# Chunk 2's first product by half products, a second order written out from slot 27 on, and stores on SyncE

## The chip, the cores and the metric

The kernel runs on one core of a Trainium2 chip. The metric is the device time of one execution in microseconds (us), the median of several runs. Below, PE is TensorE (matmuls), PEld its weight loads, DVE VectorE, ACT ScalarE, POOL GpSimd and SP SyncE; SP computes nothing and issues most of the DMAs.

## The reference

Two layers, one after the other. First a linear attention over q, k and v of shape (8 batches, 8 heads, 576 positions, 64):

```
r(x)   = max(x, 0)
phi(x) = [r(x) * cos(w_s), r(x) * sin(w_s)]        # w_s = pi/2 * s/576, 128 features
kv  = sum_s phi(k)^T v        z = sum_s phi(k)
x   = (phi(q) kv) / (phi(q) z + 1e-6)
```

Its result, with the heads side by side, is x of 4608 rows by 512. Then a gated layer with w_in (512 x 2048), beta (2048) and w_out (2048 x 512):

```
h   = x w_in
g   = h * sigmoid(beta * h)
out = g w_out
```

The output is 4608 x 512 in float32. Matmuls are in bf16 with float32 sums.

## The kernel before

**The stages.** The rows of x come in 9 chunks of 512 (number c). A batch of the attention has 576 rows, so nine blocks of 64; chunk c holds eight blocks and needs batches c and c - 1 or so. For a batch: `q_relu`, `k_relu` (L195, L199) take the ReLU of the loaded tiles, `v_scale` (L202) makes v times cos and v times sin, `kv_mm` (L270) multiplies K with V on TensorE and `kv_take` (L281) copies the result to SBUF. `q_turn_dma` (L258) transposes q by a DMA on SyncE; `q_tan` or `tan_mul` (L263, L222) multiply it by a tangent, on GpSimd or VectorE. `num_mm` (L290) makes numerators and denominators, `x_div` (L337) divides on VectorE (three short instructions, L308 to L319), and `x_turn_dma` (L365) transposes three blocks of x into the tile xt by DMAs on SyncE. For chunk 1, `x_turn_pe` (L351) transposes them on TensorE instead.

**h and out, in two ways.** Chunk c has 16 column tiles of h (jt 0 to 15). The plain way, `h_group` (L413), is four 512-column matmuls by tile (L386) and the activation by ScalarE (L394), in a bank of PSUM that holds all 512 columns. The argument `cols` of `h_mm` (L380) cuts the second to fourth of these four into narrower ones. The other way is a Strassen-like scheme with seven products where eight blocks would be multiplied (the Winograd form). `fast_ops` (L464) gives its pieces. In an order's text they are letters: 1, 5, 6, 2, 7, 3, 4 are products on TensorE; c is a copy of the first product by ScalarE to a second bank (the seed); d or D a copy to SBUF by ScalarE or VectorE; e and f are additions on VectorE; A, B, X, Y, P, Q, U, V take a finished bank. `h_pair` (L504) uses it for two column tiles of h, each product being two matmuls of 256 columns (L511); it needs four differences of xt (`x_sum`, L450) and four of w_in (`wh_sum`, L436), made by VectorE. `o_pair` (L612) uses it for half of a chunk's out, each product eight matmuls of 256 columns (L621); it needs sums of g (`g_sum`, L397, tiles S1 to S4) and differences of w_out (`w_sums`, L874). `o_fast` (L556) is an older form of the same for chunk 1 alone.

**Who uses which.** Chunk 0: h plain, out plain (`o_part`, L553). Chunk 1: h plain, out by `o_fast`. Chunk 2: h plain (`h_first`, L1037), out by `o_pair`. Chunks 3 to 8: h by `h_pair`, out by `o_pair`. The first 16 slots of the loop at L854 are chunk 0's h, slots 16 to 31 its out; `early` (L807) puts attention work at certain slots, `rest` (L763) among them at slot 4.

**What sets the order.** The kernel writes its order out by hand; every engine works through its own instructions in the order in which they are issued, and semaphores make it wait for data of another. Chunk 1 is written as Python (L882 to L936). From chunk 2's out on, a text for each chunk (`ORDERS`, L938) names one piece after another, and `chunk` (L993) issues them. In it, besides the products: s is a sum of g, t of x, W of w_in; K the K and V product, kt and kT its copy; N numerators, x the division and transpose; v, w, k, q the scaling and ReLUs of the batches ahead; g the tangent on GpSimd; TQ the transpose of q; L a load.

**SyncE's queue.** SyncE issues loads, transposes and some stores in program order; an issue that waits holds up all behind it. `store` (L532) sends 128 rows of out in two DMAs of 64 rows; for chunks 0 to 6 GpSimd issues them (L535).

The four stage tiles of 128 x 2048 floats hold w_in, then w_out as loaded; after that `wx_tiles` (L422) takes them for the differences of w_in (w and v), of xt (x) and for one tile of tangents (q).

## Time and profile before

| | |
|---|---|
| runs | 273.32, 273.35, 274.3 us; median 273.35 |
| span of the profiled execution | 272.7 us |
| of the runs' median outside that span | 0.7 us |
| TensorE clock granted | full, to three figures, in the stages from 20 to 242 us |
| DMA | 54.00 MB moved, 198 GB/s over the span |
| SyncE's queue and GpSimd's queue, share of 16 DMA engines | 59.1% and 9.6% |
| DMA issues of out by GpSimd | 58 of 128 KB, 4.5 us each to landing |
| DMA issues of out by SyncE | 10 of 128 KB, 2.4 us each to landing |

The profile is of one execution. A busy time is the union of an engine's instructions; matmuls overlap, so a TensorE that is busy all the time isn't one at its peak, and the price of a matmul is better taken from a run of many, its length divided by their number. VectorE's instructions overlap at their ends too: from one start to the next is less than the busy time of one. The chain that ended last is followed back from the end, at each step to what released the instruction. The list of waits names who waited for whom, with the sum, the count and the longest; a row of the table by stage has the length of the stage, then busy time (and instructions) of PE, PEld, DVE, ACT and POOL, the granted clock, the share of DMA engines and GB/s. A timeline row has start, length, engine, line, operation, tiles, shapes, count, and in brackets the idle time before it with who ended it.

### The profile page before, as it was taken

What the parts mean: (1) busy time and instruction counts of PE and PEld (TensorE: products, weight loads), DVE (VectorE), ACT (ScalarE), POOL (GpSimd) and SP (SyncE); (2) the same over time, 40 slices, a digit from 0 to 9 for tenths busy, and PEclk for the clock granted to TensorE, in tenths of its full rate; (3) what the DMA queues carried; (4) which work ended last, traced back from release to release, by engine and by line L of the source; (5) the groups of instructions that cost most, each with busy time, mean ns of one, the idle gap of its engine ahead of it and who ended that gap; (6) DMA issues with size and microseconds to landing.
All of it is one profiled execution on the core that took longest, in us unless ns stands there. A gap on an engine that the chain in (4) does not pass through costs nothing.

```text
span 272.7 us, 8970 instructions
## 1 busy us (share of the span) xinstructions
PE 265.3 (97%) x3712; PEld 206.8 (76%) x3712; DVE 224.0 (82%) x596; ACT 188.4 (69%) x384; POOL 68.3 (25%) x89
## 2 busy tenths in 40 slices
PE   8899999999899999999999999999999999999994
PEld 8554455455784588888888888888888888888883
DVE  5989969499989889789989997899589768757852
ACT  4778777796419656899489966996696179428920
POOL 1444000510078000660085009300840060000001
PEclk9999999999999999999999999999999999999999
DMA  6999999999969999994589439943600570015005
GB/s 237 374 395 383 392 390 319 379 201 336 284 130 311 240 348 226 240 313 103 147 216 370 92 58 223 332 71 62 181 2 2 61 185 1 2 27 130 0 2 155
DMA packets 50681, 54.00 MB, mean 198 GB/s; under 512 B 31232, under 2 KB 31760, under 8 KB 50640
## 3 DMA queue, kind: packets, MB, share of 16 engines
q1 hardware_dynamic: 47504, 45.55, 59.1%
q0 software_dynamic: 2784, 7.61, 9.6%
q8 instruction: 29, 0.48, 0.7%
q10 hardware_dynamic: 352, 0.27, 0.4%
q14 instruction: 12, 0.10, 0.1%
HBM read 36.71 MB, written 9.44 MB: 169 GB/s over the span
## 4 chain that ended last, share of the span: by engine, by line
PE 85%; DVE 9%; DMA 3%; SPq 1%; issue 1%; ACT 1%; DVEq 0%
PE ps L621 32%; PE ps L511 27%; PE ps L386 10%; PE ps L544 5%; PE ps L563 4%; PE ps L297 3%; DMA raw_v<-in_v_dram 3%; PE ps L276 3%; DVE vb L219 1%; DVE xs L319 1%; DVE qs L223 1%; SPq L79 1%; DVE S L406 1%; DVE rk L193 1%; DVE qb L193 0%
## 5 line engine op out<-in xcount | busy, mean ns | idle before, releaser
L537 POOL DMA_DIRECT2D out_dram<-o_sb x58 | 33.9, 591 | 147.3 <-ACT o_sb L658 86.3
L420 ACT ACTIVATE g_t<-ps,beta 128x512 bf16<-128x512 f32 x96 | 60.3, 702 | 1.4 <-PE ps L511 1.3
L621 PEld LDWEIGHTS <-S 128*128 128x128 bf16 x448 | 43.4, 98 | 5.2
L511 PE MATMUL ps<-w_stage 128*128 128x256 bf16 x288 | 46.6, 272 | 0.1
L386 PE MATMUL ps<-xt,win 128*128 128x512 bf16 (+1 forms) x196 | 42.8, 375 | 0.1
L511 PEld LDWEIGHTS <-w_stage 128*128 128x128 bf16 x384 | 37.3, 98 | 5.1 <-issue 0.2
L487 DVE TENSOR_TENSOR ps<-ps,p 128x256 f32<-128x256 f32 x74 | 30.5, 428 | 8.6 <-PE ps L511 3.0
L394 ACT ACTIVATE g_t<-ps,beta 128x512 bf16<-128x512 f32 x48 | 32.3, 688 | 7.2 <-PE ps L386 7.1
L621 PEld LDWEIGHTS <-g_t 128*128 128x128 bf16 x336 | 32.3, 98 | 4.5 <-ACT g_t L420 0.4
L386 PEld LDWEIGHTS <-win 128*128 128x128 bf16 x196 | 18.7, 98 | 21.1 <-issue 0.5
L511 PE MATMUL ps<-xt,win 128*128 128x256 bf16 x192 | 32.9, 273 | 0.0
L511 PEld LDWEIGHTS <-win 128*128 128x128 bf16 x288 | 28.0, 98 | 3.4
L621 PE MATMUL ps<-wout,g_t 128*128 128x256 bf16 x224 | 28.9, 273 | 0.0
L406 DVE TENSOR_TENSOR S<-g_t 128x512 bf16<-128x512 bf16 (+1 forms) x66 | 25.7, 418 | 3.3 <-ACT g_t L420 1.7
L480 ACT COPY ps<-ps 128x256 f32<-128x256 f32 x62 | 22.6, 383 | 7.5 <-PE ps L621 4.0
L217 ACT ACTIVATE vb<-raw_v,sin 128x256 bf16<-128x256 f32 (+1 forms) x58 | 26.0, 503 | 1.5 <-DMA raw_v<-in_v_dram 1.5
L621 PE MATMUL ps<-T,S 128*128 128x256 bf16 x224 | 26.6, 273 | 0.0
L621 PE MATMUL ps<-wout,S 128*128 128x256 bf16 x224 | 26.4, 273 | 0.0
L319 DVE TENSOR_TENSOR xs<-ps,rden 128x768 bf16<-128x768 f32 (+4 forms) x26 | 22.8, 884 | 0.9 <-DVE rden L312 0.2
L223 POOL TENSOR_TENSOR qs<-qt,tanr 128x1152 bf16<-128x1152 bf16 x6 | 14.3, 2387 | 27.4 <-PE ps L563 21.0
L658 ACT COPY o_sb<-ps 128x512 f32<-128x512 f32 x11 | 6.3, 587 | 20.1 <-PE ps L621 20.1
L487 DVE TENSOR_TENSOR ps<-ps,u 128x256 f32<-128x256 f32 x36 | 15.3, 427 | 5.3 <-PE ps L511 3.3
(112 smaller groups left out, 414.7 us busy)
## 6 DMA issues: line engine op xcount, KB each, us to landing
raw_v<-in_v_dram SPq DMA_DIRECT2D x7, 1152.0 KB, 9.7
raw_k<-in_k_dram SPq DMA_DIRECT2D x7, 1152.0 KB, 9.5
raw_q<-in_q_dram SPq DMA_DIRECT2D x7, 1152.0 KB, 7.4
out_dram<-o_sb POOLq DMA_DIRECT2D x58, 128.0 KB, 4.5
w_stage<-in_moe_w_in_dram SPq DMA_DIRECT2D x3, 1024.0 KB, 12.8
w_stage<-in_moe_w_out_dram SPq DMA_DIRECT2D x2, 1024.0 KB, 7.9
w_stage<-in_moe_w_out_dram SPq DMA_DIRECT2D x4, 512.0 KB, 11.9
out_dram<-o_sb SPq DMA_DIRECT2D x10, 128.0 KB, 2.4
```

The lines of the kernel that those rows point to most:

```text
L217: got = nc.scalar.activation(o, a, AF.Copy, scale=t[:, n : n + 1])
L223: return eng.tensor_tensor(dst.rearrange("q n (g p) -> q n g p", g=2), src.rearrange("q n (g p) -> q n g p", g=2), tanr[:, n0:n1].unsqueez ...
L319: nc.vector.tensor_tensor(o.rearrange("q j n s d -> q j (n s) d"), nv[:, :, a:z, :, 0:D].rearrange("q j n s d -> q j (n s) d"), rden[:, :, ...
L386: nc.tensor.matmul(ps[:, h_bank(c, jt), i * 64 : (i + w) * 64], lhsT=win[jt // 4][:, mi, (jt % 4) * P : (jt % 4 + 1) * P], rhs=xt[:, i : i ...
L394: return nc.scalar.activation(gs[c, jt // 4][:, jt % 4], ps[:, h_bank(c, jt)], AF.Silu, scale=beta[:, jt : jt + 1])
L406: return nc.vector.tensor_tensor(o, l, r, op=op)
L420: return nc.scalar.activation(gs[c, jt // 4][:, jt % 4], bank, AF.Silu, scale=beta[:, jt : jt + 1])
L480: return nc.scalar.copy(at("a", 0), at("b", 0))
L487: nc.vector.tensor_tensor(dst, at("b", 0), st["p5"], op=ALU.add)
L511: nc.tensor.matmul(dst, lhsT=l[:, g], rhs=r[:, :, g * HP : (g + 1) * HP], start=start and g == 0, stop=g == 1, skip_group_check=True)
L537: (eng or own).dma_start(out=out_v[bb, n][:, m0:m1], in_=o_sb[hf * HP : (hf + 1) * HP, m0:m1])
L621: nc.tensor.matmul(dst, lhsT=l(i), rhs=r[:, i], start=start and i == 0, stop=i == order[-1], skip_group_check=True)
```

## The change

- Chunk 2's h is made by `h_pair`, as in chunks 3 to 8. `wh_sum` now takes four column tiles at once (two pairs), so there are 16 instructions of 512 elements where there were 32 of 256. Six of them are issued in `rest`, ahead of batch 1's q ReLU; the tiles for them are taken there.
- Chunk 1's out is made by `o_pair` in place of `o_fast`.
- The loop of slots ends at 26. Slots 27 to 31 (in the text S with the tile's number; R is chunk 1's transpose on TensorE), the whole of chunk 1 (G is a plain group of h, M a difference of w_out, Z the last numerators of batch 1) and all chunks after it are texts in `ORDERS`. A number and a slash ahead of a piece mean that it belongs to another chunk, so that the end of one chunk's out stands among the beginning of the next one's h; @ names a batch. The text of every chunk is new.
- More of the ReLUs and scalings for batches ahead are single pieces that either ScalarE or VectorE takes (v, z, k, r on ScalarE; w, u, l, q on VectorE).
- Slots 5 to 11 of chunk 0's h pass `cols=2`: 21 matmuls of 512 columns become 42 of 256.
- Stores of chunks 0 to 6 are issued by SyncE in place of GpSimd.

By instructions: 512-column matmuls of h fall by 85 and 256-column ones rise by 154; GpSimd issues 2 stores in place of 58, SyncE 66 in place of 10 (besides the halves at the very end).

```diff
-            h_group(0, slot)
+            h_group(0, slot, 2 if 5 <= slot < 12 else 1)
...
-            own = (nc.gpsimd if c < 7 or (c == NTC - 1 and tt == 0) else
-                   (nc.sync, nc.scalar)[hf] if c == NTC - 1 and tt % 2 else nc.sync)
+            own = (nc.sync if c < NTC - 1 else nc.gpsimd if tt == 0 else (nc.sync, nc.scalar)[hf] if tt % 2 else nc.sync)
...
         v_scale(1, 1, n0=8)
         k_relu(1, 0, 2)
+        wx_tiles("wv")
+        for sl, kind in ((0, 1), (0, 3), (0, 2), (0, 4), (1, 1), (1, 3)):
+            wh_sum(sl, kind)
         q_relu(1, 0)
...
+    def wh_sum(sl, kind):
+        A11, A12, A21, A22 = (
+            win[sl][:, 2 * jp : 2 * jp + 2].rearrange("q g (u r f) -> q g u r f", u=2, r=2)[:, :, :, r]
+            for r in range(2) for jp in range(2))
+        s1, s2, s3, s4 = (w_sum(sl, i) for i in range(4))
...
-    for slot in range(32):
+    for slot in range(27):
...
+        0: (
+            "W23 W33 W12 Sb W21 R0 Sc Sd 1/q0@2 R1 1/M1 1/M2 1/r1@2 Se Sf 1/u5@2 1/TQ@2"),
+        1: (
+            "G0 w6@2 z7@2 M4 w1@2 G1 M3 G3 0/W31 z8@2 w3@2 G4 G2 w2@2 w0@2 u3@2 w5@2 G9 u8@2 u0@2 Gb v2@2 Ge u6@2 s10 "
+            "G8 z4@2 Lq@3 u4@2 s20 kk@2 v1@2 Gf 0/W32 u7@2 G5 Ga Z6 K02 K1 Lv@3 Gc s12 kT G7 G6 y1 y0 s40 Gd s11 N05 "
+            "N13 ox17 oy12 oxc0 r1@3 x0 oyc1 x1 ox2 s13 s22 r0@3 ox5 oy5 Lk@3 TQ oyd v7 oxd s31 z7 N23 s32 v0 s21 s42 "
+            "z4 s23 s41 oy2 w1 oy6 x2 oye ox6"),
         2: (
+            "h215 1/v6 1/s43 1/v3 1/t1 h014 1/z5 1/Lq@4 1/v8 1/t2 1/s30 1/s33 1/z6 1/oxe 0/W14 1/w2 0/W22 h113 1/oy3 "
+            "1/v4 h05 1/oy7 1/oyX 1/ox7 h15 h25 1/z3 1/t3 1/oxf h0c1 1/oyf 1/w8 h0d 1/ox3 1/u1 0/W24 1/k0 h1d h06 1/oxA "
+            "h02 h1c0 1/ox4 1/oy4 1/w0 1/v2 1/k1 1/l3 h16 h0e 1/oxY h07 1/k2 h03 h0A 1/u5 K06 1/t4 h0f K1 h1e h04 h17 "
...
+    wx_tiles("xq")
+    held = None
+    for c in range(NTC):
         for op in ORDERS[c].split():
+            other, slash, rest_ = op.partition("/")
+            held = do(int(other), rest_, held) if slash else do(c, op, held)
```

## The prediction

> **What bounds the kernel now.** I read the page's busy times and its chain first, then the chain in order of time, the list of waits, the table by stage, and last the timelines of VectorE, ScalarE and SyncE around 36 to 75 us. From the page, busy time by engine (share of the span, instructions):

> ```profile
> PE 265.3 (97%) x3712; PEld 206.8 (76%) x3712; DVE 224.0 (82%) x596; ACT 188.4 (69%) x384; POOL 68.3 (25%) x89
> ```

> The page's chain that ended last, by engine:

> ```profile
> PE 85%; DVE 9%; DMA 3%; SPq 1%; issue 1%; ACT 1%; DVEq 0%
> ```

> The same chain in order of time (start us, us, what):

> ```profile
> 45.32 1.83 PE ps L544 x8
> 47.15 0.39 PE ps L356 x7
> ...
> 69.83 0.27 ACT p L602
> ...
> 70.15 10.64 PE ps L563 x96
> 80.79 7.77 PE ps L386 x36
> 88.56 1.15 PE ps L276 x72
> ...
> 111.30 11.46 PE ps L511 x104
> ...
> 125.56 1.07 PE ps L297 x92
> ```

> From 70.15 us on the chain goes from one TensorE piece to the next, and the page gives TensorE 85% of it all. Two matmul prices follow: one of 512 columns takes 7.77 / 36 = 0.216 us, one of 256 columns 11.46 / 104 = 0.110. Ahead of 70.15 stands a ScalarE copy; the list of waits and the table by stage tell what that costs TensorE:

> ```profile
> PE ps L563 <- ACT p L602: 1.0, 1, 1.0
> ```

> ```profile
> 46.00:60.00 14.00, 14.00 (x107) 6.82 (x106) 10.02 (x25) 10.82 (x20) 4.74 (x8) 1.00 1.07 305
> 60.00:74.00 14.00, 13.04 (x291) 9.37 (x290) 13.79 (x27) 8.74 (x15) 0.00 (x0) 1.00 1.08 308
> ```

> TensorE (the first figure after the stage's length) loses 0.96 of 14 us in the second stage, at a granted clock of 1.00, in that one wait. VectorE (the third) is full there, 13.79 of 14. So after slot 27 TensorE is the bound and stands still once, and VectorE has nothing left in the very stretch to which the change adds work of its kind.

> **The change, part by part.** *Chunk 2's h.* 64 wide matmuls go (16 groups of 4), 64 x 0.216 = 13.8 us. 8 pairs of 7 half products with 2 matmuls each come: 112 x 0.110 = 12.3. All of it on the path: **-1.5 us**. [...]

> *What the pairs add elsewhere:* 16 additions on VectorE, 8 seeds on ScalarE, 8 copies on one or the other, 4 more differences of x. The differences of w_in go from 32 narrow to 16 wide ones, 6 of them moved into rest(). All of this must lie beside TensorE's work; whether VectorE has the room is worked out below.

> *The six in rest()* come ahead of a q ReLU whose data were late:

> ```profile
> 39.17 1.16 DVE L193 TENSOR_SCALAR qb<-raw_q 128x1152 bf16<-128x1152 f32 x2 [2.25 <-DMA raw_q<-in_q_dram]
> ```

> Six at 0.335 (the step of the S sums below) and a tail of 0.08 are 2.1 us, in a hole of 2.25: nothing. Had q landed earlier, they would cost up to 2.1.

> *21 matmuls in halves:* 21 x (2 x 0.110 - 0.216) = **+0.1 us**. Nothing waits for half a group, since the activation reads the whole bank.

> *Chunk 1 and the start of chunk 2 in the new order.* VectorE's prices, as steps from one start to the next in its timeline:

> ```profile
> 46.36 1.09 DVE L319 TENSOR_TENSOR xs<-ps,rden 128x896 bf16<-128x896 f32 x1
> ```

> ```profile
> 51.92 0.17 DVE L308 TENSOR_TENSOR den<-ps,eps 128x8 f32<-128x8 f32 x1 [2.46 <-PE ps L297]
> ...
> 52.97 1.42 DVE L193 TENSOR_SCALAR qb<-raw_q 128x1152 bf16<-128x1152 f32 x2
> 54.30 2.44 DVE L219 TENSOR_SCALAR vb<-raw_v,cos 128x256 bf16<-128x256 f32 x9
> 56.67 1.35 DVE L193 TENSOR_SCALAR rk<-raw_k 128x2304 bf16<-128x2304 f32 x1
> 57.94 1.40 DVE L219 TENSOR_SCALAR vb<-raw_v,sin 128x256 bf16<-128x256 f32 x5
> 59.25 1.22 DVE L876 TENSOR_TENSOR T<-wout 128x2048 bf16<-128x2048 bf16 x1
> ...
> 64.04 2.62 DVE L223 TENSOR_TENSOR qs<-qt,tanr 128x1152 bf16<-128x1152 bf16 x2
> 66.58 1.42 DVE L406 TENSOR_TENSOR S<-g_t 128x512 bf16<-128x512 bf16 x4
> 67.92 1.42 DVE L406 TENSOR_TENSOR S<-S,g_t 128x512 bf16<-128x512 bf16 x4
> 69.26 0.16 DVE L308 TENSOR_TENSOR den<-ps,eps 128x12 f32<-128x12 f32 x1
> ...
> 70.59 1.42 DVE L406 TENSOR_TENSOR S<-g_t 128x512 bf16<-128x512 bf16 x4
> ```

> ```profile
> 74.60 0.42 DVE L606 TENSOR_TENSOR o_sb<-ps,p 128x256 f32<-128x256 f32 x1
> ```

> A 512-wide sum steps 1.34 / 4 = 0.335, busy 1.42 - 3 x 0.335 = 0.415; an addition of 256 out of PSUM, busy 0.42, is taken at the same 0.335, and a PSUM copy of 512 at twice that. A scaled v steps 2.37 / 9 = 0.263; the four w_out differences take 64.04 - 59.25 = 4.79, the two tangent products 2.54, a division 70.59 - 69.26 = 1.33, the small one 52.97 - 51.92 = 1.05, K's whole ReLU 1.27, one q ReLU 0.67.

> The tight point of the new order is chunk 3's key-value product, K06 in the text of chunk 2. Between slot 26 and there the order gives VectorE 9 + 16 + 3 sums (w_in, S, x), 28 x 0.335 = 9.4; w_out 4.8; 19 scaled v, 5.0; tangents 2.5; three divisions 4.0; the small one 1.05; ReLUs 1.27 + 0.67 and a quarter of K's, 0.4; six additions and copies of 256, 2.0; two copies of 512, 1.3. Sum 32.4 us, from the end of the row at 46.36, 47.45: **79.9**. TensorE gets there with 84 wide matmuls, 18.1; 14 output products of 8 matmuls, 12.3; 9 half products of 2, 2.0; two rounds of transposes, 0.8; batch 1's last 32 numerator matmuls and batch 2's 144, at 1.07 / 92 each, 2.0; K and V 1.15. That is 36.4 from 45.3: **81.7**. VectorE has 1.8 us to spare over 34. Some of it goes: it reaches batch 1's last numerators, and batch 2's first, about 0.4 before TensorE has them. So 1 us is left, and I put **+0.3** of new waits into the sum. The ends: nothing below; above, if no instruction overlapped the tail of the one before (0.415 busy against 0.335), some 70 instructions x 0.08 = 5.6, less the 1 spare, 4.6. I take a value near the low end, since the rows above show these forms one behind another at the steps.

> *The wait that goes.* ScalarE's copy of the first output product stood behind two ReLUs of batch 3's q, and those behind a load:

> ```profile
> 67.62 2.22 ACT L192 ACTIVATE qb<-raw_q 128x1152 bf16<-128x1152 f32 x2 [0.82 <-DMA raw_q<-in_q_dram]
> ```

> In the new order one ReLU stands between the two seeds, and TensorE's next work (ox2) needs only the seed ahead of it: **-1.0 us**. What is late next is chunk 2's x (rival B).

> *Stores on SyncE.* GpSimd loses 56 issues; SyncE gains them, in order with its loads and transposes. Eight stores of chunk 0 now stand ahead of the transpose of batch 2's q. ScalarE's copies for them, SyncE's transpose as it was, and the price of an issue on SyncE (ns, least/median/most):

> ```profile
> 49.91 2.05 ACT L550 COPY o_sb<-ps 128x512 f32<-128x512 f32 x4 [1.43 <-PE ps L544]
> ```

> ```profile
> 55.47 4.65 SPq L259 DMA_TRANSPOSE qt<-qb  x1
> ```

> ```profile
> L537 SPq DMA_DIRECT2D out_dram<-o_sb x14: 466/557/597, 243.4 to 269.6; - x14
> ```

> The first copy is out at 49.91 + 2.05 / 4 = 50.4; eight issues at 0.56 end at 54.9, and the transpose started at 55.47 before: nothing. If they were not ready in a row, each us of delay is one for the tangent products behind. Later stores wait on SyncE for copies by ScalarE or VectorE and hold loads for two batches ahead, which have most of a chunk's time.

> **Sum.** The profiled execution spans 272.7 and the runs' median is 273.35, so 0.7 lies around the span. 273.35 - 1.5 + 0.1 - 1.0 + 0.3 = 271.25, **271.2**.

> **Rivals.** *A, VectorE slips and eats the gain.* For it: only 1 us is left at K06, and dependent instructions step wider (the four w_out ones at 4.79 / 4 = 1.20 against 1.22 busy). With steps 6% wider, 1.9 us, TensorE waits 0.9 more there, and as much again at the additions of chunk 2's pairs behind it: **273.0**. Against: later chunks run the same kind of pairs at 104 half products in 11.46 us.

> *B, slower: chunk 2's x arrives late through SyncE's queue.* TensorE wants the first difference of x (for h05) after 84 wide matmuls, 9 output products, 3 half products and the small pieces: 18.1 + 7.9 + 0.7 + 0.8 + 2.0 + 1.15 = 30.7, at 76.0. Now chunk 2's h begins at 80.79. VectorE comes to the end of batch 2's second division after 20.8 us of its 32.4 and the waits of 0.8, at 69.0; behind the first transpose's issue (1.2 each, if that queue is free) the second goes out by 70.2. From the view of the tile xt:

> ```profile
> DMA to landing us min/median/max: 2.3/3.0/10.5
> ```

> With the median it lands at 73.2, in time. The point from which it decides is 76.0 - 70.2 - 0.4 for the sum itself = 5.4 us; with the longest, 10.5, TensorE stands 5.1: **276.3**. For it: loads of batch 3 are issued ahead of these transposes on the same queue, and the DMA share is 1.08 in that stage. Against: the median, and that two loads stand ahead, not more. [...]

> *C, more is gained:* small waits go too and no new ones come; 0.3 less and up to 0.9 from waits under 0.3 us in the pairs of later chunks: **270.2**.

> [...]

> **How the numbers follow.** A measurement of this kernel tells 0.5%, 1.37 us, from no change: faster means below 272.0. Forecast (270.7 to 272.0) 0.48, C (down to 270.0) 0.10, A (272.0 to 274.7) 0.20, B (274.7 to 276.3) 0.21, D 0.01. Faster 0.58, same 0.20, slower 0.22. The likeliest case's own range is 270.7 to 272.0; with C, A and the larger part of B it is 270.0 to 275.7, which leaves out about 0.1.

> **What would show it.** Right: chunk 2's h as half products at 0.110 us a matmul; no TensorE gap of 1 us between 65 and 75; the third key-value product near 82; xt's transposes for chunk 2 landing within 5 us. Wrong: a TensorE wait on a difference of x or on xt near 76 (B); many waits of 0.1 to 0.5 us behind VectorE's additions between 74 and 95 (A); batch 1's q ReLU starting well after 39.2, which would say that the six sums found no hole; a store that holds SyncE while a transpose behind it is ready.

## The result and the profile after

The changed kernel takes **275.88 us** (median of 4 runs, 275.32 to 276.38) against 273.34 for the kernel before beside it (4 runs, 273.23 to 274.3): a ratio of 1.008, 95% interval 1.0062 to 1.0099, so slower by 2.5 us, under 1%. The profiled execution of the changed kernel took 275.45 us, its span is 273.6. Forecast was 271.2.

The page's busy times and the page's chain of the changed kernel, as they were shown of before:

```profile
PE 262.6 (96%) x3781; PEld 212.7 (78%) x3781; DVE 225.6 (82%) x586; ACT 200.8 (73%) x411; POOL 35.8 (13%) x33
...
PE 79%; DMA 9%; DVE 6%; issue 2%; ACT 1%; SPq 1%; POOL 0%; ACTq 0%; POOLq 0%; DVEq 0%
```

TensorE is busy 2.7 us less than before (265.3), and it is the bound as before. So the loss isn't work on TensorE: its idle time grew from 7.4 to 11.0 us. The same two stages as of before, from the table by stage:

```profile
46.00:60.00 14.00, 14.00 (x77) 6.80 (x76) 13.83 (x30) 12.50 (x22) 0.00 (x0) 1.00 1.00 323
60.00:74.00 14.00, 14.00 (x331) 10.31 (x330) 12.81 (x31) 10.21 (x20) 0.00 (x0) 1.00 1.02 227
```

The stretch into which the change puts its extra work is full: TensorE stands nowhere, and the wait of 1.0 us for ScalarE's copy is gone. The list of waits of TensorE after has instead, beside the start of the program:

```profile
PE ps L611 <- issue: 1.0, 1, 1.0
...
PE ps L502 <- DVE ps L478: 0.4, 1, 0.4
PE ps L276 <- issue: 0.3, 1, 0.3
...
PE ps L235 <- DVE qb L193: 0.2, 1, 0.2
```

"issue" is time in which TensorE waited for nothing that the profile shows. In the timeline of TensorE the long one is this:

```profile
123.45 1.70 PE L611 MATMUL ps<-T,S 128*128 128x256 bf16 x14
126.15 0.39 PE L611 MATMUL ps<-T,S 128*128 128x256 bf16 x2 [1.00 <-issue]
```

Fourteen matmuls of a product of sixteen run one behind another, TensorE stops in the middle of the product, and the last two follow. Their operands are of the same two tiles as the fourteen. No such stop of TensorE is in the trace of before at any place after its first 15 us.

The second loss stands at the end. The last rows of TensorE's timeline, before and then after:

```profile
267.95 1.04 PE L621 MATMUL ps<-wout,S 128*128 128x256 bf16 x8
```

```profile
266.77 1.04 PE L611 MATMUL ps<-T,g_t 128*128 128x256 bf16 x8
```

TensorE ends at 267.8 after and at 269.0 before, 1.2 us **earlier**; the span ends 0.9 **later** (273.6 against 272.7). From the last matmul to the end of the span it is 3.7 us before and 5.8 after. In ScalarE's timeline after:

```profile
262.77 3.41 ACTq L527 DMA_DIRECT2D out_dram<-o_sb  x2
266.30 0.58 ACT L648 COPY o_sb<-ps 128x512 f32<-128x512 f32 x1 [6.82 <-PE ps L611]
266.78 0.38 ACT L651 COPY o_sb<-ps 128x256 f32<-128x256 f32 x1
```

and in GpSimd's, before and after:

```profile
265.53 1.03 POOL L537 DMA_DIRECT2D out_dram<-o_sb  x2 [42.35 <-ACT o_sb L658]
```

```profile
267.19 1.23 POOL L527 DMA_DIRECT2D out_dram<-o_sb  x2 [70.52 <-ACT o_sb L651]
```

The text of chunk 8 now has "ox2 oyU ox7 oxf oy7 oyf ox4 oxA oxB" near its end. ScalarE issues half of the store behind oyf itself (the second of the two in its first row, issued at 265.7, when VectorE's addition is done), and only behind it comes oxA, the copy at 266.30. Its last product, ox2, was ready some 2.8 us before: run a2 below takes the copy at 264.29, with TensorE 0.8 us later there. GpSimd's two stores, which carry what oxA copies, leave 1.7 us later. All the last stores then fall together: in the trace the last five take 3.4 to 4.5 us from issue to landing, where the last five before took 2.0 to 2.5.

One number of the prediction's sum is answered too. After's four runs each took about 1.8 us more than their span, and every run below whose span is known took 1.7 to 1.9 more. The 0.7 us of the prediction (273.35 - 272.7) joined a median to the span of one execution. The profiled execution of before, of span 272.7, fits only the run of 274.3, which is 1.6 above it; an ordinary run of 273.4 then has a span of about 271.6.

### The profile page after: what moved, and what is told of

It reads as the page before. It is cut to its first block, busy times and chain, and to the rows that moved or that the text cites. A ratio compares the mean times of both kernels' runs of the same rounds, so it can differ in the third digit from the quotient of the medians.

```text
span 273.6 us, 9136 instructions
## 1 busy us (share of the span) xinstructions
PE 262.6 (96%) x3781; PEld 212.7 (78%) x3781; DVE 225.6 (82%) x586; ACT 200.8 (73%) x411; POOL 35.8 (13%) x33
## 4 chain that ended last, share of the span: by engine, by line
PE 79%; DMA 9%; DVE 6%; issue 2%; ACT 1%; SPq 1%; POOL 0%; ACTq 0%; POOLq 0%; DVEq 0%
PE ps L611 35%; PE ps L502 28%; PE ps L386 7%; DMA raw_q<-in_q_dram 6%; PE ps L297 4%; DMA raw_v<-in_v_dram 3%; PE ps L534 3%; PE ps L276 2%; DVE ps L478 1%; DVE vb L219 1%; DVE xs L319 1%; SPq L79 1%; DVE rk L193 1%; ACT g_t L416 1%; DVE o_sb L478 0%
## 5 line engine op out<-in xcount | busy, mean ns | idle before, releaser
L502 PE MATMUL ps<-w_stage 128*128 128x256 bf16 x336 | 56.5, 273 | 0.1
L611 PEld LDWEIGHTS <-S 128*128 128x128 bf16 x512 | 49.4, 98 | 7.4 <-issue 1.3
L502 PEld LDWEIGHTS <-w_stage 128*128 128x128 bf16 x448 | 43.7, 98 | 5.7 <-issue 0.4
L502 PE MATMUL ps<-xt,win 128*128 128x256 bf16 x224 | 39.8, 273 | 0.0
L611 PE MATMUL ps<-wout,S 128*128 128x256 bf16 x256 | 32.1, 273 | 0.0
L386 PE MATMUL ps<-xt,win 128*128 128x512 bf16 (+1 forms) x153 | 28.5, 345 | 0.1
L223 POOL TENSOR_TENSOR qs<-qt,tanr 128x1152 bf16<-128x1152 bf16 x6 | 14.2, 2387 | 106.3 <-PE ps L502 55.5
L406 DVE TENSOR_TENSOR S<-g_t 128x512 bf16<-128x512 bf16 x64 | 25.6, 418 | 1.6 <-ACT g_t L416 1.3
L386 PEld LDWEIGHTS <-win 128*128 128x128 bf16 x153 | 14.7, 98 | 12.1 <-issue 0.2
L319 DVE TENSOR_TENSOR xs<-ps,rden 128x768 bf16<-128x768 f32 (+4 forms) x26 | 22.8, 884 | 0.8
L502 PE MATMUL ps<-xt,w_stage 128*128 128x256 bf16 x112 | 20.7, 273 | 0.0
L502 PE MATMUL ps<-w_stage,win 128*128 128x256 bf16 x112 | 19.3, 273 | 0.4 <-DVE ps L478 0.4
L217 ACT ACTIVATE vb<-raw_v,sin 128x256 bf16<-128x256 f32 (+1 forms) x37 | 17.3, 501 | 0.9 <-DMA raw_v<-in_v_dram 0.8
```

The source lines that it names most:

```text
L217: got = nc.scalar.activation(o, a, AF.Copy, scale=t[:, n : n + 1])
L223: return eng.tensor_tensor(dst.rearrange("q n (g p) -> q n g p", g=2), src.rearrange("q n (g p) -> q n g p", g=2), tanr[:, n0:n1].unsqueez ...
L319: nc.vector.tensor_tensor(o.rearrange("q j n s d -> q j (n s) d"), nv[:, :, a:z, :, 0:D].rearrange("q j n s d -> q j (n s) d"), rden[:, :, ...
L386: nc.tensor.matmul(ps[:, h_bank(c, jt), i * 64 : (i + w) * 64], lhsT=win[jt // 4][:, mi, (jt % 4) * P : (jt % 4 + 1) * P], rhs=xt[:, i : i ...
L406: return nc.vector.tensor_tensor(o, l, r, op=op)
L502: nc.tensor.matmul(dst, lhsT=l[:, g], rhs=r[:, :, g * HP : (g + 1) * HP], start=start and g == 0, stop=g == 1, skip_group_check=True)
```

## The experiments

All times are medians beside runs of the kernel before on the same chip (273.47 to 273.57 there). The texts on record name their theories by letters. Q and P put the larger time around the span down to parts of the change (the stores, the longer program), T is the late copy at the end, S is that the wait at 69 us belongs to one execution alone, F is that TensorE waits for its own instructions, and H is that the half products save what their prices say.

### a1: the stores by GpSimd again

```diff
-            own = (nc.sync if c < NTC - 1 else nc.gpsimd if tt == 0 else (nc.sync, nc.scalar)[hf] if tt % 2 else nc.sync)
+            own = (nc.gpsimd if c < 7 or (c == NTC - 1 and tt == 0) else (nc.sync, nc.scalar)[hf] if c == NTC - 1 and tt % 2 else nc.sync)
```

> The changed kernel with one line undone: chunks 0 to 6 are stored by GpSimd again. In the two traces TensorE ends 1.2 us earlier after the change (267.8 against 269.0), the time from its end to the end of the span is 2.1 us longer (5.8 against 3.7), and what lies outside the span is 1.2 us longer (1.85 against 0.68). Theory Q: the time outside the span goes with the stores on SyncE's queue. It then falls back to 0.7, the total to about 274.7. Rival P: it goes with the longer program (69 more matmuls recorded on TensorE). It then stays at 1.8 and the total at 275.9. Neither expects the end behind the last matmul to change, since chunk 8's stores are as they were.

Measured: 281.59 us, ratio 1.0295 (1.0273 to 1.0317); profiled run 282.1, span 280.3, so 1.8 around it. Q falls: the time around the span doesn't go with the stores. Neither theory expected a total near this one: in this order SyncE's stores are worth 5.7 us (281.59 - 275.88). TensorE's waits name VectorE, two views, first TensorE's list and then VectorE's:

```profile
PE ps L502 <- DVE ps L478: 3.4, 4, 1.4
PE ps L297 <- DVE qs L223: 1.9, 1, 1.9
```

```profile
DVE qs L223 <- DMA qt<-qb: 2.4, 1, 2.4
```

For the 1.9 us the chain is whole: VectorE waits for the transpose of q, and TensorE for VectorE. The view of the tile qt says why, here of a1 and then of after (DMA to landing, least/median/most):

```profile
DMA to landing us min/median/max: 5.0/9.4/15.4
```

```profile
DMA to landing us min/median/max: 4.7/5.0/9.6
```

With the stores on another queue the transposes take 9.4 us by the median, with the stores on SyncE's own 5.0. In this order the transposes landed sooner with the stores on their own queue; why is not shown. The other 3.4 us, four waits between 118 and 207 us, were not followed back; VectorE also waits 1.6 us for loads of v and 1.1 for loads of q in this trace, against 0.3 and 0.2 in after.

### b1: the kernel before, its stores by SyncE

```diff
-            own = (nc.gpsimd if c < 7 or (c == NTC - 1 and tt == 0) else
-                   (nc.sync, nc.scalar)[hf] if c == NTC - 1 and tt % 2 else nc.sync)
+            own = (nc.sync if c < NTC - 1 else nc.gpsimd if tt == 0 else (nc.sync, nc.scalar)[hf] if tt % 2 else nc.sync)
```

> The kernel before with this one line of the change alone: chunks 0 to 6 are stored by SyncE. Theory Q: what lies outside the span rises from 0.7 to 1.8, the total to about 274.5, with TensorE's end where it was, 269.0. Rival P: outside stays 0.7, the total 273.3 unless transposes on SyncE come late behind stores, which would show as TensorE waits.

Measured: 274.09 us, ratio 1.0026 (1.0011 to 1.004): slower by 0.6 (0.3 to 1.1 by the interval). The profiled run took 275.07, its span is 273.3 (1.8 around it again, with nothing of the new order in it, so P falls as well). This run is one of the longest of the twelve. It has a stop of TensorE of the same kind:

```profile
155.16 0.27 PE L620 MATMUL ps<-T,S 128*128 128x256 bf16 x1
156.97 1.25 PE L620 MATMUL ps<-T,S 128*128 128x256 bf16 x10 [1.54 <-issue]
```

The stop came with the stores alone; the new order isn't needed for it.

### a2: the copy oxA early

```diff
-            "... oye ox2 oyU ox7 oxf oy7 oyf ox4 oxA oxB oy3 oy4 oyV oyB"),
+            "... oye ox2 oxA oyU ox7 oxf oy7 oyf ox4 oxB oy3 oy4 oyV oyB"),
```

> The changed kernel with one piece of chunk 8's text moved: ScalarE's copy of the first finished tile (oxA) stands right behind ox2 in place of behind ox4. Theory T: at the end ScalarE's queue is held by its own store, which waits for VectorE's addition until 265.7; the copy is ready about 2 us earlier but goes out at 266.3, so its two GpSimd stores start at 267.2 and fall together with the last five. With the copy ahead, the stretch from the last matmul to the end of the span shrinks from 5.8 to about 4, the total to about 274. Rival: the last stores land late (4.5 us against 2.5) because of what SyncE has queued, whatever the copy does: no change, 275.9.

Measured: 273.67 us, ratio 0.9996 (0.9977 to 1.0015): 2.2 us less than after. In ScalarE's timeline of a2, and then in GpSimd's:

```profile
264.29 0.59 ACT L648 COPY o_sb<-ps 128x512 f32<-128x512 f32 x1 [4.00 <-PE ps L611]
```

```profile
265.18 1.24 POOL L527 DMA_DIRECT2D out_dram<-o_sb  x2 [67.70 <-ACT o_sb L648]
```

The copy is 2.0 us earlier and GpSimd's stores with it; from the last matmul to the end of the span it is 3.8 us, as in the kernel before. T is shown, and its rival, late stores whatever the copy does, falls: the order of one copy and one store on ScalarE cost 2.2 us by the medians and 2.0 by the traces. The stops at "issue" are still there, 0.9 and 0.3 us in its list of waits.

### a3: chunk 0's h in whole matmuls

```diff
-            h_group(0, slot, 2 if 5 <= slot < 12 else 1)
+            h_group(0, slot)
```

> The changed kernel with slots 5 to 11 of chunk 0's h in whole 512-column matmuls again. By the price of a matmul the 21 halves cost 0.1 us, so 275.8, the same within the interval. Rival, by which the halves were to help something that the trace before does not show: slower by 0.5 or more without them.

Measured: 276.19 us, ratio 1.0096 (1.008 to 1.0111), 0.3 more than after, in another set of runs; the 21 halves cost nothing that can be told. But the stop moved. The long one was in a product of out at 124.9 us in after and is now in the key-value product at 130.4 us, as its list of waits says:

```profile
PE ps L276 <- issue: 1.0, 1, 1.0
```

Nothing near 125 us had changed; only the number of TensorE's instructions ahead was 42 smaller. That led to theory F. The trace of after has 7,562 weight loads and matmuls (3,781 of each), and the page has this line for a queue of its own (packets, MB, share of 16 engines' span):

```profile
q8 instruction: 29, 0.48, 0.8%
```

0.48 MB in 29 packets are 16 KB each, and 7,562 / 29 are 261: one packet brings some 256 instructions. Counting TensorE's loads and matmuls from the start of the program, the stops of after stand at places 3738 and 3994, exactly 256 apart, the long one of a3 at 3994, that of b1 at 4502. All are 150 to 154 beyond a multiple of 256. (The places here and in the texts on record are 28 lower than a plain count of the trace's records, at every stop alike. Distances and the fixed remainder hold; how large the remainder is depends on where the count starts.)

### b0: the kernel before once more

> The kernel before, unchanged, taken once more with a profile whose own time is known. Theory S (the trace that the prediction was read from is of the slowest of the three runs, 274.3 us, so its 1.05 us wait of TensorE for ScalarE's copy at 69 us is not in the ordinary runs, and the time outside the span is 1.8 us and not 0.7): time 273.3 to 273.6, its profiled run about 1.8 us over its span, so spans of ordinary runs near 271.6; the wait near 69 us under 0.5 us. Rival: the wait is a fixture of this order; then it is again 0.8 to 1.1 us in this trace, the ordinary span is 272.7 and 0.7 us lies outside it.

Measured: 273.57 us (10 runs), the profiled run 273.99 with a span of 272.2; the spans of the ten are 271.5 to 272.7, and each time is about 1.8 us above its span. The second stage of the table by stage, in this trace:

```profile
60.00:74.00 14.00, 13.97 (x297) 10.02 (x296) 13.79 (x25) 9.16 (x15) 0.00 (x0) 1.00 1.13 308
```

TensorE is busy 13.97 of 14 us where the trace of the prediction had 13.04. The 1.0 us wait for ScalarE's copy is not in this trace, nor in b1's. So S holds as far as these traces go: the wait belonged to the long execution of the prediction's trace, and 272.7 - 1.0 = 271.7 is the span of an ordinary run. That no ordinary run has it isn't shown, as few are traced.

### c1 and c3: the same work, the program shifted

```diff
-    warm_pe(58, 48)
+    warm_pe(15, 192)
```

(c1, on top of a2; c3 has `warm_pe(6, 464)` there and `warm_pe(1, 432, bank=2)` for `warm_pe(9, 48, bank=2)`.)

> The changed kernel with the early copy of run a2, and 43 matmuls fewer in the warm-up (15 of 192 columns in place of 58 of 48, about the same time), so that every later instruction of TensorE stands 86 places earlier in its program. In three traces TensorE stood 1.1 to 1.7 us with no releaser at places 3738, 3994, 3992 and 4502 of its loads and matmuls, all 150 to 154 beyond a multiple of 256. Theory F (TensorE waits there for its own instructions, which come in blocks of 256 by DMA): any wait of over 0.3 us without a releaser stands again 150 to 154 beyond a multiple of 256 in the new count, so not at the same matmuls as in a2 (125.75 and 131.82 us); if it finds a block with time to spare, the time falls by up to 1.5 us, 272.2 to 273.7. Rival (something at those matmuls themselves, such as their operands or the transposes running beside them): the waits stay at the same matmuls, 1.1 and 0.4 us, and the time stays 273.4 to 273.9.

> As c1, with 60 matmuls fewer in the warm-up (7 wide ones in place of 67 narrow), so 120 places. Theory F: waits without a releaser only at 150 to 154 beyond a multiple of 256 in the new count, elsewhere than in a2 and in c1; 272.2 to 274. Rival: at a2's matmuls again, 273.4 to 273.9.

Measured: c1 274.6 us, ratio 1.0036 (1.0023 to 1.0049); c3 276.81, ratio 1.0114 (1.0087 to 1.014). The stops of a2 at 126 and 132 us are gone in both. New ones came early, in c1's timeline of TensorE here:

```profile
15.59 0.19 PE L297 MATMUL ps<-kv,qs 64*64 64x65 bf16 x1
17.40 0.22 PE L297 MATMUL ps<-kv,qs 64*64 64x65 bf16 x3 [1.61 <-issue]
```

This is place 416 in the new count, 160 beyond 256, and in c3 too, where the stop is 2.7 us. So the edge is met at 150 to 160 rather than 150 to 154; but it moved with the count and not with the work, and the rival, which had the stops stay at a2's matmuls, falls. Both times were missed, by 0.9 and 2.8 us against the upper ends of F's forecasts: the shift only exchanged one late block for another. In the trace the packet of the instruction queue begins at 15.09 us in c1 and TensorE goes on 2.3 us later; in after it begins at 123.41 and TensorE goes on 2.7 us later.

c1's stop cost more than its length. The table by stage of c1:

```profile
14.00:18.00 4.00, 2.35 (x108) 1.84 (x108) 2.46 (x5) 2.50 (x7) 3.19 (x5) 0.96 1.05 402
18.00:20.00 2.00, 2.00 (x16) 0.73 (x7) 1.84 (x7) 0.52 (x2) 0.00 (x0) 0.50 1.04 386
20.00:22.00 2.00, 1.98 (x13) 1.11 (x12) 1.90 (x6) 0.72 (x2) 0.08 (x1) 0.72 1.05 387
```

The granted clock falls to 0.50 behind the stop, and wide matmuls step 0.43 us in place of 0.216. The three rows together lack (0.04 x 4 + 0.50 x 2 + 0.28 x 2) = 1.72 us of full clock, so 0.50 lasted some 3.4 us, an estimate that takes the clock as either full or 0.50 there. The mean clock of the traced run is 0.994 in c1 and in c3 (a stop of 2.7 us at the same work) and 0.988 in d2 below (a stop of 2.2 us a little earlier), against 0.998 in a2. In a2, without this stop, the clock is 1.00 in all of 14 to 24 us.

### c2: chunk 2's h plain in the new order

```diff
+        if k_ == "h" and c == 2:
+            h_plain(n, op[2], bank)
+        elif k_ == "t" and c == 1:
+            pass
...
+        for _ in range({"5": 1, "6": 1, "7": 1, "4": 1, "2": 2, "3": 2}.get(piece, 0)):
...
+            nc.tensor.matmul(ps[:, st["1" if r else "c"]],
+                             lhsT=win[jt // 4][:, mi, (jt % 4) * P : (jt % 4 + 1) * P],
+                             rhs=xt_tile(2)[:, :, jp, g * HP : (g + 1) * HP],
+                             start=(mi == 0), stop=(mi == MI - 1), skip_group_check=True)
```

(on top of a2)

> Run a2 (the changed kernel with the early copy) with chunk 2's h made plainly again, 64 matmuls of 512 columns spread over the places of the 112 half products; chunk 2's additions, seeds, copies and differences of x are left out with them. Theory H (the half products save what their prices say, 64 x 0.216 - 112 x 0.110 = 1.5 us, and VectorE's extra work is hidden): the stretch of TensorE from chunk 2's first h to its first product of out is 1.5 us longer than in a2, and the time is 275.2, if the waits for instructions do not move (they may, as 48 matmuls fewer shift the program by 96 places: 274 to 275.5). Rival (the pairs give it back through waits for VectorE, so the halves are worth nothing): 273.3 to 273.9, with TensorE's waits between 75 and 96 us gone.

Measured: 273.69 us, ratio 1.0006 (0.9991 to 1.002), as much as a2. By the time alone the rival would win. The traces say otherwise. First chunk 1's first product of out, then chunk 2's, in TensorE's timeline of a2 and then of c2:

```profile
66.92 1.26 PE L611 MATMUL ps<-wout,g_t 128*128 128x256 bf16 x10
...
94.60 1.04 PE L611 MATMUL ps<-wout,g_t 128*128 128x256 bf16 x8
```

```profile
67.08 1.16 PE L611 MATMUL ps<-wout,g_t 128*128 128x256 bf16 x9
...
95.62 1.04 PE L611 MATMUL ps<-wout,g_t 128*128 128x256 bf16 x8
```

The same work between lasts 27.68 us with the half products and 28.54 plain. In after it is 27.17 (66.58 to 93.75), in c1 27.24 (69.12 to 96.36). So the pairs gain 0.9 to 1.4 us, where 1.5 less new waits of 0.3 was forecast. c2 has no stop at "issue" (its program is 96 places shorter from chunk 2 on, so the edges fall elsewhere), and a2 has 1.2 us of them: c2 gets back there what it lost.

### d1, d2, e1, e2: trying other edges

All on top of a2. d1 cuts more of chunk 0's matmuls in halves (126 places more, from slot 4 on), d2 has whole ones and a shorter warm-up (68 places fewer), e1 cuts chunk 1's h and the S pieces in halves (136 more, after 46 us), e2 chunk 1's h alone (96 more).

```diff
d1
-            h_group(0, slot, 2 if 5 <= slot < 12 else 1)
+            h_group(0, slot, 2 if slot >= 4 else 1)
...
-            o_part(0, slot % 4, (slot - 16) // 4)
+            o_part(0, slot % 4, (slot - 16) // 4, 2)
...
-                o_mm(0, tt, (n,))
+                o_mm(0, tt, (n,), 2)
d2
-            h_group(0, slot, 2 if 5 <= slot < 12 else 1)
+            h_group(0, slot, 1)
...
-    warm_pe(58, 48)
+    warm_pe(45, 62)
e1 (e2: the first alone)
-            h_group(c, n)
+            h_group(c, n, 2)
...
-                o_mm(0, tt, (n,))
+                o_mm(0, tt, (n,), 2)
```

> Run a2 with more of chunk 0's matmuls in column halves (h from slot 4 to 15, and out from slot 16 to 23 and in the S pieces), which adds 63 matmuls; by their prices 63 x (2 x 0.110 - 0.216) = 0.25 us. TensorE's program after chunk 0 is 126 places longer, so that the edges of its blocks of 256 fall 130 places later in the work than in a2, near where run c3 had them, while nothing changes before 20 us. Theory F: the waits without a releaser at 125 and 131 us go and none comes at 15 us; 273.67 + 0.25 - 1.5 = 272.4. Rival (the blocks have nothing to do with it, longer programs only cost): 273.9.

> Run a2 with chunk 0's h in whole matmuls (42 places fewer) and 13 warm-up matmuls fewer of the same total width (26 places fewer). The edge that the work at 15 us meets moves by 26 places only; those after chunk 0 by 68, between run a3 (42, one wait of 1.09 us) and run c1 (86, none). Theory F: no wait without a releaser of over 0.3 us at 15 us, at 125 us none, at 131 us between none and 1.1 us; 272.2 to 273.2. Rival: waits at a2's matmuls, 273.6.

> Run a2 with the 48 later matmuls of chunk 1's h and the 20 of chunk 0's out in the S pieces in column halves: 68 matmuls more, 68 x 0.004 = 0.3 us by their prices, all after 46 us. The edges of the blocks of 256 stay as in a2 up to there and fall 136 places earlier in the work (as good as 120 later) from chunk 2 on, near run c3, which had no wait without a releaser after 75 us. Theory F: none at 125 and 131 us; if none comes elsewhere 273.67 + 0.3 - 1.5 = 272.5, below the kernel before; every one that comes stands 150 to 160 beyond a multiple of 256. Rival (such waits come in this order wherever the edges lie): one or two of 0.5 to 3 us elsewhere, 273.5 to 277.

> As e1 with only chunk 1's h in halves, 48 matmuls more (0.2 us): edges 96 places earlier than in a2 from chunk 2 on. Theory F as for e1: 272.4 if no edge falls where a block comes late. Rival as for e1: 273.4 to 277.

Measured: d1 278.51 us, ratio 1.0171 (1.0142 to 1.02); d2 275.63, 1.0087 (1.0061 to 1.0112); e1 273.54, 0.9998 (0.9979 to 1.0017); e2 274.66, 1.0046 (1.0028 to 1.0063). By their medians all four missed the forecast of a gain (272.2 to 273.2). d1 has its long stop in a place where no kernel had one, in TensorE's timeline:

```profile
45.99 0.44 PE L356 MATMUL ps<-ident,xs 128*128 128x128 bf16 x5
48.89 0.28 PE L356 MATMUL ps<-ident,xs 128*128 128x128 bf16 x2 [2.46 <-issue]
```

Place 1434, 154 beyond a multiple of 256. The traced run of d1, 275.51 us, is the shortest of its six; what the others lose besides, up to 3.8 us, is not shown. e1 is the other way: its profiled run, 272.73 us, has no stop, and the same product that stops in after runs through there; its program, 136 longer (7,698 in the trace), is fetched in 30 packets:

```profile
124.46 1.92 PE L611 MATMUL ps<-T,S 128*128 128x256 bf16 x16
```

```profile
q8 instruction: 30, 0.49, 0.7%
```

e1's runs lie between 272.4 and 274.5, and 4 of 12 at 272.9 or below; only the run at 272.73 is traced, so that the others have a stop is not shown. No version's median is below that of the kernel before.

The stops taken together: in the 14 traces at hand (before, after and the twelve runs), with a stop counted where TensorE's step exceeds that form's usual one by over 0.4 us, after the first 14 us and without a releaser, there are 18, in nine traces, and all 18 stand 150 to 160 places beyond a multiple of 256. (One of 0.36 us in c3 stands there too. Six smaller gaps of 0.3 to 0.4 us, at 39 to 44 us, stand elsewhere, each in chunk 0's out of a trace that lacks three or four matmul records of it; they are no stops.) So **TensorE waits at the edges of its blocks of instructions**: shown by the count and by the shifts. The size of the block is read from the trace of after: 0.48 MB in 29 packets for 7,562 loads and matmuls, and stops 256 places apart. What a late block costs stands in the runs: 0.4 to 2.9 us. The prediction did not weigh this queue.

The packets of that queue, one by one, tell more. In their order the packets belong to the edges in theirs: packet 14 of after starts at 123.41 us, and edge 14 is the stop at 126.15. The 14 traces have 395 such pairs. TensorE never passes an edge sooner than 2.2 us after the start of its packet, and at the 18 stops it goes on 2.2 to 3.2 us after that start. So it is this packet that TensorE waits for. A packet starts when TensorE is near the edge before, from 1.8 us ahead of passing it to 5.5 us behind, at the stops 0.1 to 3.8 us behind. And the stopped blocks are short: TensorE had come through them in 2.1 to 5.3 us, where the median of the others is 8.2, because the attention's narrow matmuls go by fast (72 of them in 1.22 us in a row shown further down). At all 18 stops TensorE reached the edge at most 2.2 us after its packet's start; of the other 377 edges only three were met so soon, at 2.1 to 2.2 us.

Why a packet starts late is only argued. In one block it goes with the stores: at b1's stop the packet started 3.7 us behind the edge before, in the two traces of the kernel before 0.8 and 0.6, and TensorE's work in the block took 4.3 to 4.4 us in all three. In the 5 us ahead of each of these stops the DMA share is 0.62 or more, mostly over 1, and none begins after 160 us (the share of after from 180 to 240 us is 0.34). Before and after compared, the two stages around after's stops, before first:

```profile
122.00:126.00 4.00, 4.00 (x137) 3.29 (x138) 3.93 (x13) 4.00 (x9) 0.39 (x1) 1.00 0.56 124
126.00:131.00 5.00, 5.00 (x98) 4.47 (x86) 4.73 (x14) 5.00 (x14) 0.00 (x0) 1.00 0.22 44
```

```profile
122.00:126.00 4.00, 3.15 (x116) 2.45 (x113) 3.88 (x13) 2.03 (x4) 0.00 (x0) 1.00 1.00 245
126.00:131.00 5.00, 4.85 (x125) 4.28 (x128) 3.83 (x10) 4.42 (x8) 0.00 (x0) 1.00 1.10 211
```

The DMA engines are full at 122 to 131 us after (1.00 and 1.10) and were not before (0.56 and 0.22). But a full DMA isn't enough: e1 has 0.98 at 126 to 131 and no stop, and the first 60 us are full before as after (1.01 and 1.00), with stops there in some kernels only. The three traces with GpSimd's stores (before, b0, a1) have no stop, nine of the eleven with SyncE's have one or more. Which transfers hold the packet up was not tried.

## Why the prediction was wrong, step by step

- **Chunk 2's h, -1.5 us.** Right in kind and nearly in size: 0.9 to 1.4 us by c2, waits included. The chance of 0.01 for D was for wide matmuls that are cheaper than measured. No run shows such: they step 0.216 us in the trace of before, and by c2 chunk 2's h takes longer when made of them.
- **VectorE's room (rival A) and chunk 2's x (rival B).** Right. Two rows of TensorE's timeline after:

```profile
75.72 0.38 PE L502 MATMUL ps<-w_stage 128*128 128x256 bf16 x2
...
81.93 1.22 PE L276 MATMUL ps<-vb,rk 64*64 64x130 bf16 x72
```

  The first use of a difference of x was forecast at 76.0 and came at 75.7, the third key-value product at 81.7 and came at 81.9, neither behind a wait. Sums by steps from start to start hold over 35 us.
- **The six sums in rest().** Right: batch 1's q ReLU starts 0.1 us later than before, and TensorE's wait behind it is 0.2 us after; of the kernel before, b0's list has 0.6 and the first trace's none:

```profile
39.28 1.16 DVE L193 TENSOR_SCALAR qb<-raw_q 128x1152 bf16<-128x1152 f32 x2
```

- **The 21 halves, +0.1 us.** Too small to tell (a3).
- **"The wait that goes", -1.0 us, and "0.7 lies around the span".** Wrong, and one mistake. The wait did go, as the stage at 60 to 74 us shows, but b0's trace of the kernel before doesn't have it either. The prediction took the wait off a median that, by b0, did not hold it. The 0.7 was the sign: with some 1.8 around every span, the profiled execution was the longest of the three runs.
- **"Stores on SyncE: nothing."** Wrong. The queue was argued through for the transposes, which in fact became faster (11.3 us to landing before, 5.0 after); that TensorE's own instructions come by DMA was not in the sum. With the order as it is, the two stops cost 1.3 us by the list of waits. They go with the stores: b1 has a stop with the stores alone, a1 has none with the new order and GpSimd's stores (and loses more elsewhere).
- **The end.** Wrong. The sum took the time behind the last matmul as unchanged, without a word, though the text of chunk 8 is new. The late copy cost 2.2 us (a2).

With these terms the sum closes: 271.2 + 1.0 (a wait that wasn't there) + 2.2 (the late copy) + 1.3 (the stops of the traced run) = 275.7, measured 275.88. e1's traced run, with neither of the last two, took 272.73; less 0.3 for its 68 halves that is 272.4, where the prediction without its false -1.0 says 272.2. That is one of the shorter runs of e1, whose median is 273.54. The measured time lies near rival B's 276.3 by chance alone: chunk 2's x was in time.

## What to carry to other kernels

Before a wait of the trace is taken off the median, look whether the traced execution is a median one: its span against those of other runs, or a second trace. At the end of a program, look for an engine that both copies and issues stores: here it did them in order, so a copy behind a store that waited was 2.0 us late (after against a2), and so were the stores behind that copy. Where TensorE stops in the middle of a product with no releaser, count its instructions and look at the packets of its instruction queue: here a stop at a fixed remainder of 256 (150 to 160, all 18) was a late block of its program. It moves when the length of the program ahead of it changes, so that a small edit far from the place cost 1 to 5 us by the median here (c1, c3, d1, d2, e2 against a2), and none of those tried gained.
